# A fused cross-attention and token-mixing kernel rewritten: casting loads, state read in head groups under a mask, keys made per token, three batches in one loop

## The chip, the cores and the metric

The kernel runs on one core of a Trainium2 chip. The metric is the device time of one execution in microseconds, as the median of several runs. A profile is one more execution, with the hardware's own record of every instruction; its span goes from the first to the last instruction on the core.

## What is computed

Inputs are x (8 batches, 8 heads, 512 tokens, 64 wide), state (8, 8, 32, 64) and three weight matrices. First comes attention both ways between x and state, for each batch and head; then the two results are put together into 544 tokens of 512 features, and these are mixed across tokens.

```python
scores = scale * x @ state.T                      # 512 x 32 for each head
a = softmax(scores, over the 32 state rows)
xread = a @ state                                 # 512 x 64
a2 = softmax(scale * state @ x.T, over the 512 tokens)
sread = a2 @ x                                    # 32 x 64
y = concat([xread, sread]) as 544 x 512           # heads side by side
wq, wk = y @ w_q, y @ w_k                         # 544 x 64
mixed = (scale * wq @ wk.T) @ y                   # 544 x 512
out = relu(mixed) @ w_out                         # 544 x 512
```

## The kernel before, in words

No softmax subtracts its maximum. One exponent E serves both directions: summed over state rows and divided it gives A, the weights of xread; multiplied with x and a column of ones it gives sread and its sums. xread itself is never formed. Since it is A times state, the kernel multiplies state with w_q and w_k once (SW) and A^T with that. In the mixing, wk^T y (64 x 512, "V") is made first, through G, the product of A and the keys, and a block-diagonal state "stbd"; then mixed = wq V.

Setup, before the batches: w_out, w_q and w_k come in by SP's queue as f32 (L66 to L76), and GpSimd casts them to bf16 (L67, L80, L81). For each batch state comes as 32 partitions (L85), ScalarE casts it (L87), VectorE writes its eight blocks into stbd one by one (L94, 64 copies in all), and TensorE transposes it and multiplies it with the weights (L102 to L134).

Then a loop over eight batches, each written as one straight line. x comes in as f32 (L141, 1 MB a batch, tokens on partitions). VectorE casts it twice: x_sd with a column of ones for sread (L143, L147) and x_sd2 with pairs of heads side by side (L152). TensorE transposes that 16 times (L157), ScalarE copies the result (L163, L164), 16 matmuls make the scores pt_ps (L169). ScalarE takes the exponent E_sn (L177), VectorE sums and inverts (L179, L181), GpSimd multiplies to A_sn (L183). Eight transposes make A^T (L193, copied at L199); 32 matmuls of 65 columns make sread head by head (L206), which VectorE normalises (L217, L218) and TensorE transposes (L227, L233). Then wqk (L237, L245: queries and keys at once, feature layout, copied at L253), the keys turned back by five transposes (L258, L263, copied at L269, L270), g (L275, L283), v (L286, L290, V at L298), four mixS and four narrow mixT32 matmuls (L303, L310) with relu to rmix (L317, L324), sixteen fin matmuls of 512 columns (L336, copied at L343) and one output of 1 MB (L344). After every fourth batch the 32 state tokens of four batches go through w_out together (L352 to L361).

Tiles double up (pool pb has two buffers of each), and the tile framework sets all waits and the order on each engine: it takes instructions in the order written, and lets a ready one of the next batch ahead where an engine and a buffer are free. `nc.any` copies go to ScalarE or VectorE at its choice. The instruction order below is what it made.

Of the kernel before, what the change touches and what calls it, by code (L numbers as in the profile page):

```python
# [8 lines left out]
FP = mybir.dt.float32  # L10
BF = mybir.dt.bfloat16
AF = mybir.ActivationFunctionType
ALU = mybir.AluOpType
# [4 lines left out]
def kernel(  # L18
# [14 lines left out]
    SP = S + NS  # L33
    DH = moe_w_q.shape[1]
    NG = 4
    SG = S // NG
    KC = DM // 128
    HG = H // 4
    NP = H // 2
    scale = 1.0 / float(D) ** 0.5  # L40
# [3 lines left out]
    persist = ctx.enter_context(tc.tile_pool(name="persist", bufs=1))  # L44
    pb = ctx.enter_context(tc.tile_pool(name="pb", bufs=2))
    rmixp = ctx.enter_context(tc.tile_pool(name="rmixp", bufs=1))
    outstg = ctx.enter_context(tc.tile_pool(name="outstg", bufs=3))
    psA = ctx.enter_context(tc.tile_pool(name="psA", bufs=2, space=bass.MemoryType.PSUM))
    psB = ctx.enter_context(tc.tile_pool(name="psB", bufs=1, space=bass.MemoryType.PSUM))
    psC = ctx.enter_context(tc.tile_pool(name="psC", bufs=3, space=bass.MemoryType.PSUM))  # L50

    ident = const.tile([128, 128], BF, name="ident")
    make_identity(nc, ident)
    ident64hi = const.tile([128, 64], BF, name="ident64hi")
    nc.gpsimd.memset(ident64hi, 0.0)
    make_identity(nc, ident64hi[64:128, :], nomemset=True)

    state_sb = []
    stbd_sb = []
    stT2_sb = []  # L60
    SW_sb = []

    with tc.tile_pool(name="wstage", bufs=1) as wstage:
        w_out_sb = persist.tile([128, KC, DM], BF, name="w_out_sb")
        wo_stage = wstage.tile([128, KC, DM], FP, name="wo_stage")
        nc.sync.dma_start(out=wo_stage, in_=moe_w_out.rearrange("(k p) e -> p k e", p=128))  # L66
        nc.gpsimd.tensor_copy(out=w_out_sb, in_=wo_stage)  # L67

        w_qk_sb = persist.tile([128, NP, 2 * DH], BF, name="w_qk_sb")
        wq_stage = wstage.tile([128, NP, DH], FP, name="wq_stage")  # L70
        wk_stage = wstage.tile([128, NP, DH], FP, name="wk_stage")
        nc.sync.dma_start(
            out=wq_stage,
            in_=moe_w_q.rearrange("(q2 hp d) j -> hp d q2 j", q2=NP, hp=2),
        )
        nc.sync.dma_start(  # L76
            out=wk_stage,
            in_=moe_w_k.rearrange("(q2 hp d) j -> hp d q2 j", q2=NP, hp=2),
        )
        nc.gpsimd.tensor_copy(out=w_qk_sb[:, :, 0:DH], in_=wq_stage)  # L80
        nc.gpsimd.tensor_copy(out=w_qk_sb[:, :, DH : 2 * DH], in_=wk_stage)  # L81

        for b in range(B):
            stf = wstage.tile([NS, H, D], FP, name="stf", tag="stf", bufs=2)
            nc.sync.dma_start(out=stf, in_=state[b].rearrange("h n d -> n h d"))  # L85
            st_sb = persist.tile([NS, H, D], BF, name=f"state_sb{b}")
            nc.scalar.copy(out=st_sb, in_=stf)  # L87
            state_sb.append(st_sb)

            stbd = persist.tile([128, HG, 4 * D], BF, name=f"stbd{b}")  # L90
            nc.gpsimd.memset(stbd, 0.0)
            for h in range(H):
                g, k = h // 4, h % 4
                nc.vector.tensor_copy(  # L94
                    out=stbd[32 * k : 32 * k + 32, g, D * k : D * k + D],
                    in_=st_sb[:, h, :],
                )
            stbd_sb.append(stbd)

            stT2_ps = psC.tile([128, NP, NS], BF, name="stT2_ps", tag="psC")  # L100
            for q in range(NP):
                nc.tensor.transpose(  # L102
                    out=stT2_ps[:, q, :],
                    in_=st_sb[:, 2 * q : 2 * q + 2, :],
                    identity=ident[0:NS, 0:NS],
                )
            stT2 = persist.tile([128, NP, 2 * NS], BF, name=f"stT2_sb{b}")
            nc.gpsimd.memset(stT2, 0.0)
            nc.any.tensor_copy(out=stT2[0:64, :, 0:NS], in_=stT2_ps[0:64, :, :])
            nc.any.tensor_copy(  # L110
                out=stT2[64:128, :, NS : 2 * NS], in_=stT2_ps[64:128, :, :]
            )
            stT2_sb.append(stT2)

            swt_ps = psC.tile([128, NP, 2 * NS], FP, name="swt_ps", tag="psC")
            for q in range(NP):
                nc.tensor.matmul(  # L117
                    out=swt_ps[:, q, :],
                    lhsT=w_qk_sb[:, q, :],
                    rhs=stT2[:, q, :],  # L120
                    start=(q == 0),
                    stop=(q == NP - 1),
                )
            swt = wstage.tile([128, NP, 2 * NS], BF, name="swt", tag="swt", bufs=2)
            nc.any.tensor_copy(out=swt, in_=swt_ps)
            sw_ps = psC.tile([128, HG, 2 * DH], BF, name="sw_ps", tag="psC")
            for g in range(HG):
                nc.tensor.transpose(
                    out=sw_ps[:, g, :],
                    in_=swt[:, 2 * g : 2 * g + 2, :],  # L130
                    identity=ident,
                )
            sw = persist.tile([128, HG, 2 * DH], BF, name=f"SW_sb{b}")
            nc.any.tensor_copy(out=sw, in_=sw_ps)  # L134
            SW_sb.append(sw)

    rmix = rmixp.tile([128, KC, B * SP], BF, name="rmix")

    for b in range(B):
# [3 lines left out]
        nc.vector.tensor_copy(  # L143
            out=x_sd[:, :, :, 0:D],
            in_=xf32.rearrange("p h (c d) -> p h c d", c=NG),
        )
        nc.gpsimd.memset(x_sd[:, :, :, D : D + 1], 1.0)  # L147
        x_sd2 = pb.tile([128, NG, 2 * D * NP], BF, name="x_sd2")
        x_sd2_v = x_sd2.rearrange("p c (q hp d) -> p c q hp d", q=NP, hp=2)
        xf32_v = xf32.rearrange("p (q hp) (c d) -> p c q hp d", q=NP, hp=2, c=NG)  # L150
        for hp in range(2):
            nc.vector.tensor_copy(out=x_sd2_v[:, :, :, hp, :], in_=xf32_v[:, :, :, hp, :])  # L152

        xT_ps = psA.tile([128, NP, NG, SG], BF, name="xT_ps", tag="psA")
        for q in range(NP):
            for c in range(NG):
                nc.tensor.transpose(  # L157
                    out=xT_ps[:, q, c, :],
                    in_=x_sd2[:, c, 128 * q : 128 * q + 128],
                    identity=ident,  # L160
                )
# [230 lines left out]
```

## Time and profile before

| | us |
|---|---|
| runs | 183.29 median (182.05 to 183.35, 3 runs) |
| profiled execution, span | 179.0 |
| TensorE busy | 126.7 (71%) |
| ScalarE busy | 90.2 (50%) |
| VectorE busy | 69.5 (39%) |
| GpSimd busy | 31.2 (17%) |
| mean granted TensorE clock | 0.82 |

Busy time of TensorE includes the time that a pipelined matmul is under way, so it is not work at full rate. "PEclk" is the clock granted to TensorE, in tenths of full speed or as a share. In groups, "idle before" is the time that the engine stood free just before these instructions, and what ended it.

### The profile page before, as it was taken

To read this page: it belongs to the slowest core of one execution; us is meant where nothing else is said; L and a number is where in the kernel's file an instruction comes from. 1 tells how busy PE (TensorE), PEld (TensorE's weight loads), DVE (VectorE), ACT (ScalarE), POOL (GpSimd) and SP (SyncE) were. 2 spreads that over 40 slices of the span, in tenths; PEclk is the share of its full clock that TensorE was granted. 3 is DMA by queue.
4 is the path that set the end of the run, shared out by engine and by line. 5 is a ranking of instruction groups with operands and counts; after the bars stand their busy time and mean duration, and the time that the engine had idled before them with its cause. 6 is when DMAs were issued, how large, how long until landed. Compare 5 with 4: busy or idle time off the path is not lost.

```text
span 179.0 us, 2649 instructions
## 1 busy us (share of the span) xinstructions
PE 126.7 (71%) x1064; PEld 68.4 (38%) x1064; DVE 69.5 (39%) x172; ACT 90.2 (50%) x159; POOL 31.2 (17%) x43
## 2 busy tenths in 40 slices
PE   0020656689995897699679967996899789848800
PEld 0010535464254434443453345445535533522300
DVE  0099979985616403440434043404140350203000
ACT  2130574477465744663477446744666673543600
POOL 3592003100411040004302130033021004000000
PEclk9999999999999759756995795579558975975985
DMA  5992071076019303900580061005000500320061
GB/s 148 302 275 94 15 247 25 12 234 224 17 59 302 111 0 156 296 17 4 205 264 0 4 240 53 0 4 234 0 0 4 234 0 2 150 88 0 29 222 42
DMA packets 13507, 19.29 MB, mean 108 GB/s; under 512 B 3512, under 2 KB 11704, under 8 KB 12472
## 3 DMA queue, kind: packets, MB, share of 16 engines
q1 hardware_dynamic: 13496, 19.14, 31.8%
q8 instruction: 8, 0.13, 0.3%
q14 instruction: 3, 0.02, 0.0%
HBM read 10.22 MB, written 8.91 MB: 107 GB/s over the span
## 4 chain that ended last, share of the span: by engine, by line
PE 56%; DVE 18%; ACT 13%; DMA 3%; issue 3%; POOL 1%; SPq 1%; ACTq 0%; DVEq 0%; POOLq 0%
PE fin_ps L336 23%; DVE stbd L94 8%; PE mixS_ps L303 7%; PE srd_ps L206 6%; DMA stf<-in_state_dram 3%; DVE x_sd L143 3%; DVE sread_sb L218 3%; PE pt_ps L169 3%; ACT E_sn L177 3%; PE xT_ps L157 3%; PE at_ps L193 2%; PE v_ps L286 2%; ACT xT_sb L163 2%; PE v_ps L290 2%; ACT wqkT_sb L253 2%
## 5 line engine op out<-in xcount | busy, mean ns | idle before, releaser
L336 PE MATMUL fin_ps<-w_out_sb,rmix 128*128 128x512 bf16 x128 | 42.2, 501 | 0.0
L343 ACT COPY ostage<-fin_ps 128x512 f32<-128x512 f32 x32 | 18.8, 586 | 23.3 <-PE fin_ps L336 23.0
L183 POOL TENSOR_TENSOR A_sn<-E_sn,rinv 128x1024 bf16<-128x1024 bf16 x8 | 15.5, 1941 | 76.0 <-DVE rinv L181 75.0
L336 PEld LDWEIGHTS <-rmix 128*128 128x128 bf16 x128 | 15.0, 124 | 26.7 <-issue 20.7
L94 DVE COPY stbd<-state_sb 32x64 bf16<-32x64 bf16 x64 | 17.5, 274 | 10.5 <-POOL w_qk_sb L81 9.1
L217 DVE RECIPROCAL rinv<-srd_ps 32x4 f32<-32x4 f32 x16 | 2.6, 161 | 46.5 <-PE srd_ps L206 46.5
L303 PE MATMUL mixS_ps<-wqkT_sb,V_sb 64*128 64x512 bf16 x32 | 17.4, 587 | 1.3 <-ACT V_sb L298 1.2
L317 ACT ACTIVATE rmix<-mixS_ps 128x512 bf16<-128x512 f32 x23 | 13.6, 597 | 5.0 <-PE mixS_ps L303 4.3
L206 PE MATMUL srd_ps<-x_sd,E_sn 128*32 128x65 bf16 x256 | 14.0, 210 | 1.7 <-ACT E_sn L177 1.4
L317 DVE TENSOR_SCALAR rmix<-mixS_ps 128x512 bf16<-128x512 f32 x9 | 6.2, 692 | 21.1 <-PE mixS_ps L303 21.1
L206 PEld LDWEIGHTS <-E_sn 128*32 128x32 bf16 x256 | 10.7, 105 | 7.0 <-issue 3.5
L152 DVE CAST x_sd<-xf 128x1024 bf16<-128x1024 f32 x16 | 10.8, 680 | 6.3 <-PE xT_ps L157 6.3
L147 POOL MEMSET x_sd<- 128x32 bf16 x8 | 6.4, 821 | 37.7 <-PE srd_ps L206 37.7
L157 PE MATMUL xT_ps<-ident,x_sd 128*128 128x128 bf16 x128 | 12.3, 254 | 0.0
L169 PE MATMUL pt_ps<-stT_sb,xT_sb 128*128 128x64 bf16 x128 | 8.9, 224 | 3.0 <-ACT xT_sb L163 2.9
L179 DVE TENSOR_REDUCE rsum<-E_sn 128x32 f32<-128x1024 bf16 x8 | 9.7, 1211 | 1.2 <-ACT E_sn L177 1.2
L143 DVE CAST x_sd<-xf 128x2048 bf16<-128x2048 f32 x8 | 9.6, 1204 | 0.0
L233 ACT COPY srT_sb<-srT_ps 128x128 bf16<-128x128 bf16 x8 | 2.1, 266 | 14.5 <-PE srT_ps L227 14.5
L157 PEld LDWEIGHTS <-x_sd 128*128 128x128 bf16 x128 | 9.2, 114 | 0.3
L102 PE MATMUL stT_ps<-ident,state_sb 32*128 32x32 bf16 x32 | 2.3, 188 | 10.0 <-POOL w_qk_sb L81 9.0
L163 ACT COPY xT_sb<-xT_ps 128x1024 bf16<-128x1024 bf16 x8 | 8.1, 1012 | 1.8 <-PE xT_ps L157 1.8
L117 PE MATMUL swt_ps<-stT_sb,w_qk_sb 128*128 128x64 bf16 x32 | 3.1, 239 | 8.1 <-ACT stT_sb L110 8.1
(67 smaller groups left out, 158.1 us busy)
## 6 DMA issues: line engine op xcount, KB each, us to landing
xf<-in_x_dram SPq DMA_DIRECT2D x8, 1024.0 KB, 5.7
out_dram<-ostage SPq DMA_DIRECT2D x8, 1024.0 KB, 3.9
wo_stage<-in_moe_w_out_dram SPq DMA_DIRECT2D x1, 1024.0 KB, 5.5
stf<-in_state_dram SPq DMA_DIRECT2D x8, 64.0 KB, 2.1
out_dram<-ostage SPq DMA_DIRECT2D x2, 256.0 KB
wq_stage<-in_moe_w_q_dram SPq DMA_DIRECT2D x1, 128.0 KB, 5.6
wk_stage<-in_moe_w_k_dram SPq DMA_DIRECT2D x1, 128.0 KB, 5.7
```

The costliest lines, as they stand in the source:

```text
L94: nc.vector.tensor_copy(out=stbd[32 * k : 32 * k + 32, g, D * k : D * k + D], in_=st_sb[:, h, :],)
L143: nc.vector.tensor_copy(out=x_sd[:, :, :, 0:D], in_=xf32.rearrange("p h (c d) -> p h c d", c=NG),)
L152: nc.vector.tensor_copy(out=x_sd2_v[:, :, :, hp, :], in_=xf32_v[:, :, :, hp, :])
L157: nc.tensor.transpose(out=xT_ps[:, q, c, :], in_=x_sd2[:, c, 128 * q : 128 * q + 128], identity=ident,)
L163: nc.any.tensor_copy(out=xT_sb[:, 0:2], in_=xT_ps[:, 0:2])
L169: nc.tensor.matmul(out=pt_ps[:, c, 2 * q : 2 * q + 2, :], lhsT=xT_sb[:, q, c, :], rhs=stT2_sb[b][:, q, :], start=(q == 0 and c % 2 == 0), ...
L183: nc.gpsimd.tensor_tensor(out=A_sn, in0=E_sn, in1=rinv[:, :, :, None].to_broadcast((128, NG, H, NS)), op=ALU.mult,)
L206: nc.tensor.matmul(out=srd_ps[:, g, 65 * hh : 65 * hh + 65], lhsT=E_sn[:, c, h, :], rhs=x_sd[:, h, c, :], start=(hh == 0 and c == 0), stop ...
L303: nc.tensor.matmul(out=mixS_ps, lhsT=V_sb[:, 128 * k : 128 * k + 128], rhs=wqT_sb[:, 0:S], start=True, stop=True,)
L317: nc.any.tensor_scalar(out=rmix[:, k, S * b : S * b + S], in0=mixS_ps, scalar1=0.0, scalar2=None, op0=ALU.max,)
L336: nc.tensor.matmul(out=fin_ps, lhsT=rmix[:, k, S * b + SG * c : S * b + SG * c + SG], rhs=w_out_sb[:, k, :], start=(k == 0), stop=(k == KC ...
L343: nc.any.tensor_copy(out=ostage[:, c, :], in_=fin_ps)
```

## The change

The kernel is written anew, with the same arithmetic. On the inputs:

- x (two loads a batch, four heads each), w_q, w_k and w_out are loaded by GpSimd's queue, and the transfer casts them from f32 to bf16. All of x has its own place in SBUF (x_bf0 to x_bf7), and all 19 loads are issued at the start. State comes in one load of 128 partitions. All casts of x on VectorE and of weights on GpSimd are gone.
- state's copies, transposes and stbd are made for all batches at once, with head h = 4r + q at partition group q of half r: four stbd copies, sixteen transposes, four weight products of 512 columns.

In a batch:

- s_xT transposes x_bf with two tokens of a group of four side by side, so no copy in another layout is needed; s_pt multiplies with state in two interleaved copies. VectorE, not ScalarE, copies xT and A^T.
- s_srd multiplies the E of four heads with x of four heads and a block of ones: eight matmuls of 128 x 320 in place of 32 of 32 x 65. Only the blocks on the diagonal are wanted: VectorE multiplies by the inverse sum and a mask in one scalar_tensor_tensor. s_srT sums over partition groups by a stacked identity, as it transposes.
- s_wqk makes queries in feature layout as before, and keys directly per token, by twelve matmuls of 64 columns; the five transposes back are gone.
- s_mix takes queries of real and state tokens together, 2 x 272 columns, so the narrow matmuls and their relu are gone. fin's results leave in pairs of token groups: copies of 1024 columns, all on ScalarE, and outputs of 512 KB.

The loop runs over ten iterations. Iteration i works on batch X = i (xT, pt, srd), Y = i - 1 (at, srT, wqk, g, v) and Z = i - 2 (mix, fin), and the stages of the three are written between one another. PSUM is two pools, psA with three tiles of two banks and psB with two of one.

GpSimd's queue, from the start of the program to the second A ("[waits ...]" names the semaphores; DMASW0 to DMASW7 count the landings of loads, taken in turn). Before:

```order
L67 CAST w_out_sb<-wo_stage 128x2048
L80 CAST w_qk_sb<-wq_stage 128x4x64
L81 CAST w_qk_sb<-wk_stage 128x4x64
...
L147 MEMSET x_sd 128x32 x3
L183 TENSOR_TENSOR A_sn<-E_sn,rinv 128x1024 x2
```

Now:

```order
L66 DMA x_bf_73<-in_x_dram 128x4x256 x2
L75 DMA w_qk<-in_moe_w_q_dram 128x4x64
L78 DMA w_qk<-in_moe_w_k_dram 128x4x64
...
L83 DMA w_o<-in_moe_w_out_dram 128x4x512
L66 DMA x_bf_75<-in_x_dram 128x4x256
L66 DMA x_bf_75<-in_x_dram 128x4x256 [waits DMASW0_49]
L66 DMA x_bf_76<-in_x_dram 128x4x256 [waits DMASW1_49]
...
L66 DMA x_bf_80<-in_x_dram 128x4x256 [waits DMASW2_49]
L194 TENSOR_TENSOR A<-E,rinv 128x1024 [waits DVE_49,Activation_49] x2
```

The loads moved from SP's queue to GpSimd's, ahead of every A; from the ninth load on each one waits for the landing of the load eight before it.

ScalarE's queue over one batch of the steady part. Before:

```order
L199 COPY AT_sb<-at_ps 128x1024
L233 COPY srT_sb<-srT_ps 128x128
L253 CAST wqkT_sb<-wqk_ps 128x544
L163 COPY xT_sb<-xT_ps 128x1024
L270 COPY wkt_sb<-wkt_ps 32x64
L164 COPY xT_sb<-xT_ps 128x1024
L298 ACTIVATE V_sb<-v_ps 64x512
L177 ACTIVATE E_sn<-pt_ps 128x1024
L317 ACTIVATE rmix<-mixS_ps 128x512
L324 ACTIVATE rmix<-mixT_ps 128x4x32
L317 ACTIVATE rmix<-mixS_ps 128x512 x2
L343 COPY ostage<-fin_ps 128x512 x4
```

Now:

```order
L344 ACTIVATE rmix<-mix_ps 128x544 x3
L185 ACTIVATE E<-pt_ps 128x1024
L274 CAST wq<-wq_ps 64x544
L367 COPY ost<-fin_ps 128x1024
L328 ACTIVATE V<-v_ps 64x512
L367 COPY ost<-fin_ps 128x1024
```

The copies of A^T, xT, srT and keys left ScalarE for VectorE; the exponent of batch X now stands between the relu and the outputs of batch Z, and V of batch Y between the two outputs.

TensorE in one steady iteration now stands so (counts of matmuls in a row): 8 xT, 2 mix, 6 at, 2 mix, 8 xT, 2 at, 4 mix, 4 srT, 16 pt, 4 fin, 6 wq, 12 wk, 4 fin, 8 srd, 2 fin, 8 g, 2 fin, 3 v, 4 fin.

The core of the diff:

```diff
-        xf32 = pb.tile([128, H, NG * D], FP, name="xf32")
-        nc.sync.dma_start(out=xf32, in_=x[b].rearrange("h (p c) d -> p h c d", c=NG))
-        x_sd = pb.tile([128, H, NG, D + 1], BF, name="x_sd")
...
+    psA = ctx.enter_context(tc.tile_pool(name="psA", bufs=3, space=bass.MemoryType.PSUM))
+    psB = ctx.enter_context(tc.tile_pool(name="psB", bufs=2, space=bass.MemoryType.PSUM))
+    x_bf = [xin.tile([128, 2, NP + 1, NC * D], BF, name=f"x_bf{b}") for b in range(B)]
...
+    def load_x(b):
+        for r in range(2):
+            nc.gpsimd.dma_start(
+                out=x_bf[b][:, r, 0:NP, :],
+                in_=x[b, NP * r : NP * r + NP].rearrange("h (p c) d -> p h (c d)", c=NC),
+            )
+
+    nc.sync.dma_start(
+        out=st_f, in_=state.rearrange("b (r q) n d -> (q n) (b r) d", r=2)
+    )
+    load_x(0)
...
+    load_x(1)
+    nc.gpsimd.dma_start(out=w_o, in_=moe_w_out.rearrange("(k p) e -> p k e", p=128))
+    for b in range(2, B):
+        load_x(b)
...
+    nc.vector.tensor_copy(
+        out=st_bf, in_=st_f[:, :, :, None, :].to_broadcast((128, B, 2, 2, D))
+    )
...
+    def s_xT(b):
...
+                nc.tensor.transpose(
+                    out=ps[:, u, h, :],
+                    in_=x_bf[b][:, h // NP, h % NP, 128 * u : 128 * u + 128],
+                    identity=ident,
+                )
+            nc.vector.tensor_copy(out=xT[:, u], in_=ps[:, u])
...
+    def s_srd(b):
...
+            for c in range(NC):
+                nc.tensor.matmul(
+                    out=ps,
+                    lhsT=L["E"][:, c, r, :, :],
+                    rhs=x_bf[b][:, r, :, D * c : D * c + D],
+                    start=(c == 0),
+                    stop=(c == NC - 1),
+                )
+            nc.vector.reciprocal(out=rinv2[:, r : r + 1], in_=ps[:, NP, 0:1])
+            nc.vector.scalar_tensor_tensor(
+                out=sbd[:, r, :, :],
+                in0=ps[:, 0:NP, :],
+                scalar=rinv2[:, r : r + 1],
+                in1=mask[:, :, None].to_broadcast((128, NP, D)),
+                op0=ALU.mult,
+                op1=ALU.mult,
+            )
...
+    def s_wqk(b):
...
+        for c in range(NC):
+            for r in range(2):
+                nc.tensor.matmul(
+                    out=psk[:, c, :],
+                    lhsT=L["AT"][:, r, c, :],
+                    rhs=sw[:, b, r, DH : 2 * DH],
+                    start=(r == 0),
+                    stop=(r == 1),
+                )
...
+    def s_mix(b, k, eng):
+        L = live[b]
+        ps = psA.tile([128, 2, 512], FP, name="mix_ps", tag="psA")
+        for h in range(2):
+            nc.tensor.matmul(
+                out=ps[:, h, 0:HALF],
+                lhsT=L["V"][:, 128 * k : 128 * k + 128],
+                rhs=L["wq"][:, HALF * h : HALF * h + HALF],
+                start=True,
+                stop=True,
+            )
...
+    for i in range(B + 2):
+        X, Y, Z = i, i - 1, i - 2
+        hx, hy, hz = X < B, 0 <= Y < B, 0 <= Z
+        if hx:
+            s_xT(X)
+        if i == 0:
+            setup_sw()
+        if hz:
+            s_mix(Z, 0, "act")
+            s_mix(Z, 1, "dve")
+        if hy:
+            s_at(Y)
+        if hz:
+            s_mix(Z, 2, "act")
+            s_mix(Z, 3, "act")
+            nc.gpsimd.tensor_copy(out=rmix_s[:, Z // 4, :, Z % 4, :], in_=rmix[:, Z, :, S:SP])
+        if hx:
+            s_pt(X)
+        if hz:
+            s_fin_mm(Z, 0)
+        if hy:
+            s_srT(Y)
+            s_wqk(Y)
+        if hz:
+            s_fin_mm(Z, 1)
+            s_fin_out(Z, 1, "act")
+        if hx:
+            s_srd(X)
+        if hy:
+            s_g(Y)
+        if hz:
+            s_fin_mm(Z, 2)
+        if hy:
+            s_v(Y)
+        if hz:
+            s_fin_mm(Z, 3)
+            s_fin_out(Z, 3, "act")
+            if Z % 4 == 3:
+                s_fin_s(Z // 4)
```

More of the change, by code (lines that the diff above doesn't have):

```diff
@@ L131 @@
                     identity=ident,
                 )
[L133 to L139, printed above, removed]
[L140 to L156 removed]
+        stT_v = stT_ps.rearrange("p b r (q n) -> p b (r q) n", q=NP)
@@ new lines, in s_v @@
+    def s_v(b):
+        L = live[b]
+        ps = psB.tile([DH, 2, NP, D], FP, name="v_ps", tag="psB")
+        nc.tensor.matmul(
+            out=ps, lhsT=L["wk"][:, NC, :], rhs=L["sbd"], start=True, stop=False
+        )
+        for r in range(2):
+            nc.tensor.matmul(
+                out=ps[:, r, :, :],
+                lhsT=L["G"][:, r, :],
+                rhs=stbd[:, b, r, :, :],
+                start=False,
+                stop=(r == 1),
+            )
+        V = work.tile([DH, DM], BF, name="V")
+        nc.scalar.mul(out=V, in_=ps.rearrange("p r q d -> p (r q d)"), mul=float(scale2))
+        L["V"] = V
```

460 lines of the change are left out of this document (212 added, 248 removed).

## The prediction

> **What bounds the kernel now.** I read the page first: engines, slices, chain.
>
> ```profile
> span 179.0 us, 2649 instructions
> ...
> PE 126.7 (71%) x1064; PEld 68.4 (38%) x1064; DVE 69.5 (39%) x172; ACT 90.2 (50%) x159; POOL 31.2 (17%) x43
> ...
> PEclk9999999999999759756995795579558975975985
> ...
> GB/s 148 302 275 94 15 247 25 12 234 224 17 59 302 111 0 156 296 17 4 205 264 0 4 240 53 0 4 234 0 0 4 234 0 2 150 88 0 29 222 42
> ...
> HBM read 10.22 MB, written 8.91 MB: 107 GB/s over the span
> ...
> PE 56%; DVE 18%; ACT 13%; DMA 3%; issue 3%; POOL 1%; SPq 1%; ACTq 0%; DVEq 0%; POOLq 0%
> ```
>
> No engine is full. TensorE is busiest, at 71%, and holds 56% of the chain; VectorE and ScalarE hold 31% more, though they are busy only 39% and 50%. So it is not one engine's work that ends last but a chain that passes from engine to engine. The GB/s row falls near zero between bursts, so DMA bounds nothing. The clock row dips again and again from the fourteenth slice on.
>
> Next the chain in order of time, for one batch:
>
> ```profile
> 120.67 0.45 PE at_ps L193 x8
> 121.12 0.92 PE srd_ps L206 x25
> ...
> 128.76 0.56 PE v_ps L290 x2
> 129.33 0.87 PE pt_ps L169 x14
> ...
> 133.11 4.63 PE fin_ps L336 x16
> 137.74 0.45 PE at_ps L193 x8
> ```
>
> Five more rows of the chain, for the steps on the start, the clock and the end below:
>
> ```profile
> 0.73 0.45 SPq L66
> ...
> 2.32 5.99 DMA stf<-in_state_dram
> ...
> 29.97 1.92 POOL A_sn L183
> ...
> 47.22 4.48 PE fin_ps L336 x14
> ...
> 168.41 0.88 PE fin_ps L352 x4
> ```
>
> From at_ps to the next at_ps is 17.07 us: the period of one batch. From at_ps to the end of v_ps (129.3) the chain hops through attention copies, key transposes, g and v in 8.7 us. Only one batch's fin_ps, 4.63 us, is dense work. Eight such periods are three quarters of the span. Last I read the period in stretches of 3.4 us (columns: stretch, length, then busy time and count for PE, PEld, DVE, ACT, POOL, granted clock, DMA share, GB/s):
>
> ```profile
> 118.20:121.60 3.40, 3.40 (x37) 1.99 (x36) 0.00 (x0) 2.65 (x5) 0.00 (x0) 1.00 0.00 0
> 121.60:125.00 3.40, 1.96 (x32) 1.27 (x29) 2.11 (x5) 0.88 (x2) 1.38 (x1) 1.00 0.74 308
> 125.00:128.40 3.40, 2.53 (x30) 1.85 (x26) 0.76 (x3) 2.64 (x3) 0.00 (x0) 0.50 0.00 0
> 128.40:131.80 3.40, 3.30 (x27) 1.71 (x26) 1.04 (x2) 2.10 (x4) 0.00 (x0) 0.50 0.00 0
> 131.80:135.20 3.40, 3.40 (x12) 1.12 (x12) 1.13 (x2) 1.38 (x4) 1.91 (x1) 0.50 0.00 0
> 135.20:138.60 3.40, 3.40 (x35) 2.00 (x34) 0.00 (x0) 2.58 (x5) 0.00 (x0) 0.99 0.02 5
> ```
>
> A stretch with PE busy 1.96 of 3.40 us (58%) is followed by three at clock 0.50; after two nearly full ones (3.30 and 3.40) it is 1.00 again. The hand-overs cost twice: as idle time, and as half speed afterwards, when the next dense work comes.
>
> **The change part by part.** *Steady state.* In each iteration three batches stand between one another on TensorE, so one batch's hand-over is filled by another's matmuls. What is left is TensorE's own time. Paces at full clock:
>
> ```profile
> 166.00:169.30 3.30, 2.40 (x11) 0.88 (x9) 1.00 0.00 0
> ```
>
> This row is fin_ps (L336) alone, busy time and count of PE and PEld, then clock: 11 matmuls of 512 columns in 2.40 us, 0.218 each, so 0.43 ns a column. A 128-column transpose is at_ps's 0.45 / 8 = 0.056, and a small one srd_ps's 0.92 / 25 = 0.037 (both rows above). An iteration after has: 16 xT, 8 at and 4 srT of 128 columns, 28 x 0.056 = 1.57; 16 pt, 12 wk, 8 g and 4 narrow wq, 40 x 0.037 = 1.48; 2 wq, 0.44; v, 0.44; 8 srd of 320 columns (they replace 32 of 65), 8 x 0.136 = 1.09; 8 mix of 272, 8 x 0.116 = 0.93; 16 fin, 3.49. Sum 9.44 us.
>
> The other engines, by the groups of instructions on ScalarE, on VectorE and on GpSimd (the last two numbers ahead of the idle time are busy us and mean ns):
>
> ```profile
> L177 ACT ACTIVATE E_sn<-pt_ps 128x1024 bf16<-128x1024 f32 x8 | 8.2, 1024 | 1.0 <-PE pt_ps L169 1.0
> L163 ACT COPY xT_sb<-xT_ps 128x1024 bf16<-128x1024 bf16 x8 | 8.1, 1012 | 1.8 <-PE xT_ps L157 1.8
> ...
> L253 ACT CAST wqkT_sb<-wqk_ps 128x544 bf16<-128x544 f32 x8 | 4.9, 612 | 2.7 <-PE wqk_ps L245 2.7
> ...
> L298 ACT ACTIVATE V_sb<-v_ps 64x512 bf16<-64x512 f32 x8 | 4.7, 591 | 7.6 <-PE v_ps L290 7.6
> ```
>
> ```profile
> L179 DVE TENSOR_REDUCE rsum<-E_sn 128x32 f32<-128x1024 bf16 x8 | 9.7, 1211 | 1.2 <-ACT E_sn L177 1.2
> L143 DVE CAST x_sd<-xf 128x2048 bf16<-128x2048 f32 x8 | 9.6, 1204 | 0.0
> L218 DVE TENSOR_TENSOR sread_sb<-srd_ps,rinv 32x256 bf16<-32x256 f32 x16 | 6.5, 407 | 0.3
> L317 DVE TENSOR_SCALAR rmix<-mixS_ps 128x512 bf16<-128x512 f32 x9 | 6.2, 692 | 21.1 <-PE mixS_ps L303 21.1
> L181 DVE RECIPROCAL rinv<-rsum 128x32 f32<-128x32 f32 x8 | 2.8, 352 | 0.7
> ...
> L164 DVE COPY xT_sb<-xT_ps 128x1024 bf16<-128x1024 bf16 x1 | 0.7, 680 | 0.0
> ```
>
> ```profile
> L183 POOL TENSOR_TENSOR A_sn<-E_sn,rinv 128x1024 bf16<-128x1024 bf16 x8 | 15.5, 1941 | 76.0 <-DVE rinv L181 75.0
> ```
>
> ScalarE per iteration: exponent 1.02, wq 0.61, V 0.59, three rmix of 544 at 0.61, two output copies of 1024 at 1.01: 6.1 us. VectorE: three bf16 copies at 0.68, sum 1.21, reciprocal 0.35, two head-group reads at 0.41 (scalar_tensor_tensor is new; the nearest row is L218) with two small reciprocals, at most 0.35 together, srT and rmix at about 0.69, and wk and G of 320 and 128 columns, by the share of columns 0.43 and 0.17: 6.4 to 6.9 us. The three casts of x (1.20 and two half-size ones) are gone; they lay on the chain as "x_sd". GpSimd: 1.94 and a small copy. All three stay under 9.4, so TensorE bounds, and those removals are worth nothing beyond that.
>
> TensorE still waits where three two-bank tiles go round through xT, mix, pt and fin: the mix tiles wait for relu. Below: about 0.3 an iteration, one wait. Above: 2.4 us, the difference of 17.07 and the most that the engine stood free in a period (1.44 + 0.87 + 0.10 us in the six stretches). I take 1.0, since three mix hand-overs remain and the rest has other matmuls between. Iteration: 10.4 us. What hides the hand-overs of wk, g and v are fin's four groups, which stand between them; without that cover each costs what it does now, 8.7 us in all, and V, for which all mix waits, would be late next.
>
> *Clock.* 9.44 of 10.4 us is 91% busy, far from the 58% that was followed by half clock. But the program starts at half speed: the fourteen fin_ps at 47.2 us took 0.32 each, against 0.22 at clock 1.00, though the page's clock row shows 9 there. The first dense work in the new order meets it too: two stretches at half speed, about 7 us, lose 3.5. [...] The rows above show two busy ones at 0.50 before 1.00, so 3.5 stands.
>
> *Start.* State comes in one load, and x and the weights come cast, in 19 loads that GpSimd issues. Its first A stands behind all 19; and loads 9 to 19 each wait until the load eight before has landed. So A(0) waits for load 11: x of four batches 4.19 MB, the weights 1.31, and state's 0.52 beside them on another queue, 6.0 MB. How fast casting loads run, no row shows. The nearest are the first ten us (columns as above) and the loads' time from issue to landing:
>
> ```profile
> 0.00:10.00 10.00, 0.28 (x4) 0.18 (x4) 0.94 (x1) 2.86 (x5) 5.09 (x16) 1.00 0.86 242
> ```
>
> ```profile
> xf<-in_x_dram SPq DMA_DIRECT2D x8, 1024.0 KB, 5.7
> ...
> stf<-in_state_dram SPq DMA_DIRECT2D x8, 64.0 KB, 2.1
> ```
>
> The first ten us moved 242 GB/s; one x load alone, 1.05 MB in 5.7 us, 184. I take the middle, 213: 28.2 us. With 1 us to the first issue, 2.1 for a small landing, 0.5 for the last issue and 1.94 for A, A(0) stands at 34 us. Bounds: 308 GB/s (a stretch above) gives 25; 150, should the cast cost a quarter or GpSimd's issue take longer than SP's 0.45, gives 46 to 48. The data chain itself is done sooner: state landed at 8.3 us before (the row at 2.32); its cast 1.2, sixteen transposes at half speed 1.8, copies out of PSUM near 2.2, two of xT 1.4, pt 0.9, exponent 1.0, sum 1.2, reciprocal 0.35 and some 2 us of hand-overs end near 20. So the queue sets the start. Casting on arrival saves nothing here: before, A(0) was ready at 31.9 (the row at 29.97). Later x is no limit: 10.22 MB at 213 is in at 51 us, and x(7) is wanted near 98.
>
> [...]
>
> *Iteration 1* is A(0) to V(0), the 8.7 us chain, at half clock without its x_sd: 9. *Iteration 8* lacks xT, pt and srd (0.90 + 0.59 + 1.09): 7.8. *Iteration 9* has mix, three relus in line on ScalarE (0.3 + 1.83 + 0.2), fin 3.49 and the last group 0.87: 7. *Tail*: before, PE ends at 169.3 and the span at 179.0, 9.7 us; the last transfer is now half as large, 0.5 MB at 222 GB/s less, so 8 with what hangs on it.
>
> Sum: 34 + 9 + 6 x 10.4 + 3.5 + 7.8 + 7 + 8 = 131.8 us of span. The median of the runs, 183.29, is 4.3 over the profiled span. 131.8 + 4.3 = **136 us**.
>
> **The rivals.** *Slow casting loads.* If a casting packet takes twice as long (106 GB/s), A(0) stands at 62 and the time is 136 + 28 = 164. For it: 16-bit targets make packets of 512 B, and no row has a cast. Against: the read, 1 KB, is what it was.
>
> *The clock keeps falling.* mix, xT and at carry short matmuls and relu waits together. If one window each iteration falls under the mark, two at half speed follow: 3.4 us lost, 6 x 3.4 = 20, time 156. For it: 58% is close to what that section may reach with waits of 2 us. Against: one such wait is 0.3.
>
> *Loads bound everything, slower than before.* Casting element by element: x(7) must be in by 183.3 - 4.3 - (10.4 + 7.8 + 7 + 8) = 146 us, so the mechanism decides from 10.2 MB / 146 = 70 GB/s down. At 60 it is 170 + 33 + 4 = 207 us. Against: it takes a fourfold loss.
>
> *The three batches do not overlap*, the order holding one stage for the next as now: 34 + 9 + 6 x 17.1 + 14.5 (17.1 less 2.6) + 9.5 (fin partly at half speed) + 8 + 4.3 = 182 us. Against: no stage's input is made less than two groups of matmuls ahead.
>
> **How the numbers follow.** Forecast 0.65, slow loads 0.12, falling clock 0.13, loads bound 0.05, no overlap 0.05. Forecast's own range: start -9 / +14, waits 7 x (-0.7 / +1.4), not both at their ends, 124 to 154. To hold 8 in 10 it runs from 122 to 162, into the falling clock and slow loads. Faster by over 1% (what a measurement of this kernel can just tell from nothing): the first three, 0.90. Within 1%: no overlap, 0.05. Slower: 0.05.
>
> **What would show it.** The first A on GpSimd near 32, behind 19 loads; TensorE's period near 10.4 with clock 1.00 from about 50 us; fin_ps near 0.22 each; ScalarE and VectorE near 6 to 7 us a period; about 8 us after the last matmul. Wrong would be: GpSimd free well before the sum is ready, a clock row with 5s past the middle, or a gap before xT for want of x.

## The result, and the profile after

Measured beside each other, the changed kernel took 119.35 us (118.86 to 119.63, 4 runs) and the kernel before 183.12 us (182.05 to 183.35, 4 runs): ratio 0.654, 95% interval 0.649 to 0.658. The forecast was 136.0, with 122 to 162 as range. The direction was right; the time lies below the range.

The page of the changed kernel, the same rows as before:

```profile
span 117.8 us, 2155 instructions
...
PE 91.4 (78%) x884; PEld 54.4 (46%) x884; DVE 67.3 (57%) x138; ACT 57.4 (49%) x80; POOL 33.1 (28%) x41
...
PEclk9999999999999999999999999999999999999955
...
GB/s 73 199 155 188 202 196 196 196 196 195 37 0 6 17 161 178 6 178 132 46 58 125 178 0 181 171 58 43 178 178 6 178 81 97 149 213 32 333 53 27
...
q0 software_dynamic: 10032, 4.85, 31.3%
...
PE 70%; DVE 17%; ACT 2%; issue 2%; POOL 2%; ACTq 0%; DVEq 0%; POOLq 0%
```

TensorE alone now holds 70% of the chain (56% before), and ScalarE, which held 13%, holds 2%. The clock row has no dip until the work is done; that the start ran at half speed (0.47 us for a matmul of 512 columns at 17.55) it does not show (see the cold clock below). One period of the steady state (columns as in the prediction):

```profile
53.07:63.22 10.15, 10.15 (x109) 5.95 (x106) 6.52 (x13) 5.87 (x8) 2.20 (x2) 1.00 0.26 105
```

TensorE is busy in all of a period of 10.15 us, at clock 1.00; VectorE 6.5, ScalarE 5.9, GpSimd 2.2. That is the forecast's picture (10.4; 6.4 to 6.9; 6.1; about 2.2). Where it went otherwise most is the start. The chain in order of time up to the first A:

```profile
3.89 1.78 DVE stbd L93
...
9.50 0.48 DVE x_bf L95
...
9.98 1.43 DVE st_bf L102
...
11.46 1.05 PE stT_ps L110 x8
12.53 0.29 DVE stT L117
...
17.55 1.86 PE swT_ps L132 x4
19.41 0.33 PE sw_ps L146 x2
19.74 0.80 PE pt_ps L177 x15
20.54 1.49 PE sw_ps L146 x14
...
24.99 0.33 DVE rinv L192
...
25.46 1.92 POOL A L194
```

and GpSimd's own queue, its last load and that A (in brackets its idle time and what ended it):

```profile
20.39 0.74 POOL L66 DMA_DIRECT2D x_bf<-in_x_dram  x1 [0.66 <-DMA x_bf<-in_x_dram]
25.46 1.91 POOL L194 TENSOR_TENSOR A<-E,rinv 128x1024 bf16<-128x1024 bf16 x1 [4.33 <-DVE rinv L192]
```

GpSimd was through with its 19 loads at 21.1 us and then stood idle 4.33 us for the sum, one of the signs of being wrong that the prediction had named. So the data chain set the start, not the queue. On that chain VectorE filled stbd and then the eight columns of ones (4.3 us for the eight, the last at 9.50) before it cast the state at 9.98. The stT copies, which alternate between VectorE and ScalarE, ran from 12.5 to 17.5 us with the two copies of xT(0) between them. Then the set-up's own matmuls (swT, and sixteen transposes to sw) stood ahead of the last of the sixteen pt matmuls until 22.0.

The forecast's terms against the profile (A(0) ready; A(0) to the first mix; six periods with the clock's loss; iterations 8 and 9; the tail after TensorE's last matmul):

| term | forecast | measured | difference |
|---|---|---|---|
| start, A(0) ready | 34 | 27.4 | -6.6 |
| iteration 1, to 34.3 | 9 | 6.9 | -2.1 |
| six iterations, to 94.7 | 62.4 + 3.5 | 60.4 | -5.5 |
| iteration 8, to 102.7 | 7.8 | 8.0 | +0.2 |
| iteration 9, to 109.0 | 7 | 6.3 | -0.7 |
| tail, to 117.8 | 8 | 8.8 | +0.8 |
| median over profiled span | 4.3 | 1.6 | -2.7 |

### The profile page after: what moved, and what is told of

It is laid out like the page before. It is cut to its first block, busy times and chain, and to the rows that moved or that the text cites. A ratio compares the mean times of both kernels' runs of the same rounds, so it can differ in the third digit from the quotient of the medians.

```text
span 117.8 us, 2155 instructions
## 1 busy us (share of the span) xinstructions
PE 91.4 (78%) x884; PEld 54.4 (46%) x884; DVE 67.3 (57%) x138; ACT 57.4 (49%) x80; POOL 33.1 (28%) x41
## 3 DMA queue, kind: packets, MB, share of 16 engines
q1 hardware_dynamic: 4632, 9.44, 21.3%
## 4 chain that ended last, share of the span: by engine, by line
PE 70%; DVE 17%; ACT 2%; issue 2%; POOL 2%; ACTq 0%; DVEq 0%; POOLq 0%
PE fin_ps L356 25%; PE mix_ps L335 8%; PE xT_ps L163 6%; PE srd_ps L221 6%; PE wq_ps L258 3%; PE at_ps L207 3%; DVE x_bf L95 3%; PE pt_ps L177 3%; PE v_ps L316 2%; DVE xT L168 2%; PE wk_ps L278 2%; DVE rsum L190 2%; PE srT_ps L243 2%; POOL A L194 2%; PE swT_ps L132 2%
## 5 line engine op out<-in xcount | busy, mean ns | idle before, releaser
L356 PE MATMUL fin_ps<-w_o,rmix 128*128 128x512 bf16 x128 | 34.0, 381 | 0.0
L194 POOL TENSOR_TENSOR A<-E,rinv 128x1024 bf16<-128x1024 bf16 x8 | 15.3, 1910 | 25.4 <-DVE rinv L192 17.9
L367 ACT COPY ost<-fin_ps 128x1024 f32<-128x1024 f32 x16 | 16.2, 1012 | 9.3 <-PE fin_ps L356 7.8
L163 PE MATMUL xT_ps<-ident,x_bf 128*128 128x128 bf16 x128 | 11.6, 237 | 9.4 <-DMA x_bf<-in_x_dram 7.3
L344 ACT ACTIVATE rmix<-mix_ps 128x544 bf16<-128x544 f32 x24 | 14.1, 623 | 6.0 <-PE mix_ps L335 6.0
L168 DVE COPY xT<-xT_ps 128x1024 bf16<-128x1024 bf16 x16 | 10.9, 684 | 9.4 <-PE xT_ps L163 9.4
L66 POOL DMA_DIRECT2D x_bf<-in_x_dram x16 | 12.8, 806 | 5.3 <-DMA x_bf<-in_x_dram 2.7
L190 DVE TENSOR_REDUCE rsum<-E 128x32 f32<-128x1024 bf16 x8 | 9.8, 1220 | 5.5 <-ACT E L185 5.5
L335 PE MATMUL mix_ps<-wq,V 64*128 64x272 bf16 x64 | 10.8, 279 | 0.7 <-ACT ost L367 0.6
L185 ACT ACTIVATE E<-pt_ps 128x1024 bf16<-128x1024 f32 x8 | 8.2, 1024 | 5.9 <-PE pt_ps L177 5.8
L221 PE MATMUL srd_ps<-x_bf,E 128*128 128x320 bf16 x64 | 10.2, 299 | 0.0
## 6 DMA issues: line engine op xcount, KB each, us to landing
x_bf<-in_x_dram POOLq DMA_DIRECT2D x16, 256.0 KB, 10.4
```

The source lines that it names most:

```text
L66: nc.gpsimd.dma_start(out=x_bf[b][:, r, 0:NP, :], in_=x[b, NP * r : NP * r + NP].rearrange("h (p c) d -> p h (c d)", c=NC),)
L163: nc.tensor.transpose(out=ps[:, u, h, :], in_=x_bf[b][:, h // NP, h % NP, 128 * u : 128 * u + 128], identity=ident,)
L168: nc.vector.tensor_copy(out=xT[:, u], in_=ps[:, u])
L185: nc.scalar.activation(out=E, in_=ps.rearrange("p c r (q n) -> p c r q n", q=NP), func=AF.Exp, scale=float(scale))
L190: nc.vector.reduce_sum(out=rsum, in_=Ev, axis=AX.X)
L194: nc.gpsimd.tensor_tensor(out=A.rearrange("p c r q n -> p (c r q) n"), in0=Ev, in1=rinv[:, :, None].to_broadcast((128, NC * 2 * NP, NS)), ...
```

## The experiments

The theory going in: the interleaving of three batches is the gain; it fills the hand-overs and keeps the clock. The rival: the new instructions (casting loads, wider and fewer matmuls) are the gain. Beside it stood the misses: what sets the start, and what the cold clock costs.

### Less interleaving

The first run keeps every stage and writes them batch after batch:

```
-    for i in range(B + 2):
-        X, Y, Z = i, i - 1, i - 2
+    for b in range(B):
+        s_xT(b); s_pt(b); s_at(b); s_srd(b); s_srT(b); s_wqk(b)
+        s_g(b); s_v(b); s_mix(b, 0, "act"); ...; s_fin_mm(b, c)
```

> The changed kernel's stages unchanged (casting loads, masked read, token-layout keys, same instructions), but written batch after batch, so that TensorE does no work of another batch while a batch's chain of copies runs. Theory (the interleaving of three batches is most of the gain): TensorE waits some 7 to 8 us in each batch for E, A, AT, wk, G, V and rmix; the period goes from 10.15 to 17 to 19 us and the clock leaves 1.00 again: 165 to 190 us. Rival (the shorter and fewer instructions are the gain, the order is worth little): period 11 to 12 us, 125 to 135 us.

The second has two batches in the loop: all attention of batch i, with mix and fin of batch i - 1 between.

```
-        X, Y, Z = i, i - 1, i - 2
+        X, Z = i, i - 1
```

> The changed kernel with a loop over two batches in place of three: the attention of a batch, from xT to V, in one iteration, and only mixing and output of the batch before as filling work. Theory (overlap sets the period): the chain of one batch, about 5.5 us of TensorE and some 7 us of copies between, no longer fits into 10.15 us, of which the other batch fills about half of the gaps: period 11.5 to 13 us, one iteration less: 125 to 138 us. Rival (TensorE alone sets the period, any second batch fills the gaps): period 10.2 and one iteration less at the end: 112 to 118 us.

Measured: batch after batch 217.3 us (ratio to before 1.192, interval 1.184 to 1.200), two batches 145.8 us (0.802, 0.796 to 0.808). The first went past the theory's own range, the second is above it by 8 us; both are far from the rival. The page of the first:

```profile
span 215.6 us, 2144 instructions
...
PE 127.5 (59%) x876; PEld 70.1 (33%) x884; DVE 72.4 (34%) x138; ACT 58.1 (27%) x80; POOL 33.1 (15%) x41
...
PEclk9999999957887576958597666958596767858595
```

Against the changed kernel, TensorE is busy 36.1 us longer with the same matmuls (127.5 less 91.4) and idle 61.7 us longer (88.1 less 26.4). Together that is the whole difference of the spans, 97.8: by estimate from these two numbers a bit over a third is half clock, the rest idle hand-overs. (The mean granted clock is 0.776 against 0.974, and the same matmuls are busy longer: fin 41.2 us against 34.0, srd 18.7 against 10.2, mix 14.5 against 10.8.) How the one makes the other, in stretches of 3.4 us (laid so that the changes of the clock in the trace fall on their bounds):

```profile
112.20:115.70 3.50, 1.25 (x24) 1.00 (x23) 1.19 (x3) 1.02 (x1) 0.00 (x0) 0.99 0.55 174
115.70:119.10 3.40, 0.00 (x0) 0.00 (x0) 1.36 (x2) 0.00 (x0) 1.79 (x1) 0.50 0.15 59
119.10:122.50 3.40, 3.22 (x18) 2.13 (x18) 1.36 (x4) 0.00 (x0) 0.12 (x1) 0.50 0.00 0
```

After a stretch with TensorE busy 1.25 us the clock is 0.50; while E, its sum and A are made TensorE does nothing; the dense stretch after it (3.22 us) still runs at 0.50. And by groups, the same 128 matmuls of fin:

```profile
L356 PE MATMUL fin_ps<-w_o,rmix 128*128 128x512 bf16 x120 | 41.2, 501 | 1.4 <-ACT rmix L344 1.3
```

501 ns each, as in the kernel before, against 381 in the changed one (below). The two-batch loop, one of its periods:

```profile
45.73:59.32 13.59, 10.87 (x106) 6.18 (x105) 6.59 (x13) 5.80 (x9) 2.20 (x2) 1.00 0.19 77
```

In this period the clock stays at 1.00, and 2.7 us of 13.6 are idle. V(0) starts at the same time as in the changed kernel (33.4 and 33.6 us), V(7) 27.8 us later (129.5 and 101.8): the whole difference. So the gain needs the interleaving: without it the new instructions are slower than the kernel before. The other half of the comparison, the old instructions in the interleaved order, was not run. As TensorE's own work fills the period now, its shorter matmuls may have a share in the gain that is not shown.

### The start

Two set-up moves. First the ones columns leave the set-up:

```
-    for b in range(B):
-        nc.vector.memset(x_bf[b][:, :, NP, :], 1.0)
...
+        nc.vector.tensor_scalar(out=x_bf[b][:, :, NP, :], in0=xT[:, 1, 0:4, :]...,
+            scalar1=0.0, scalar2=1.0, op0=ALU.mult, op1=ALU.add)
```

> The eight memsets of the ones columns (4.3 us on VectorE ahead of the state's cast) are taken out of the set-up; each batch's ones are made from its xT copy instead, as x times 0 plus 1, in its own iteration. Theory (VectorE's set-up chain, state cast to stT to swT to pt(0) to A(0), sets the start, not GpSimd's load issues): the state's cast starts at about 5.7 instead of 9.9 us, the stT copies then wait for ScalarE's stbd casts, which end at 10.5, instead of 12.85: A(0) starts 2 to 4.3 us earlier, end 115 to 117.5 us. Rival (the sixteen loads on GpSimd's queue, free at 21.1 us, or their arrival set the start): less than 1 us, 118.5 to 119.5.

Then, on top of it, ScalarE's stbd casts go behind pt(0):

```
-        nc.scalar.copy(out=stbd[blk, :, :, q, :], in_=st_f[blk])
...
+        nc.scalar.activation(out=stbd[blk, :, :, q, :], in_=st_f[blk], func=AF.Copy, scale=one[blk])
```

> As the run before, and ScalarE's four stbd casts (4.2 us and ahead of its stT copies) wait for a scalar made from sw, so that they follow pt(0)'s exponential. Theory (the data chain): stT, swT and pt(0) come 4 to 6 us earlier than in the changed kernel, until GpSimd's queue of loads, free at 21.1 us, takes over as the bound: A(0) starts at 21.1 instead of 25.5 us, end about 114 to 116 us. Rival (the loads' arrival or the clock, opened later by the set-up's thinner window, gives it back): 117 to 119.5 us.

Measured: 117.6 us each (ratios 0.644, 0.638 to 0.651; and 0.646, 0.640 to 0.652). The first is the theory's direction, just past its range: A(0) began at 22.83 in place of 25.46. The second gained nothing more, as its rival said. Its chain in order of time shows why:

```profile
10.51 10.47 DMA x_bf<-in_x_dram
...
21.27 0.17 POOL x_bf L66
...
22.02 1.93 POOL A L205
24.00 0.64 PE at_ps L218 x8
```

and the stretches behind it:

```profile
22.20:25.60 3.40, 1.27 (x21) 1.12 (x22) 2.85 (x5) 3.01 (x4) 1.74 (x1) 1.00 1.47 201
25.60:29.10 3.50, 3.50 (x27) 2.14 (x26) 2.00 (x4) 0.92 (x2) 0.00 (x0) 0.51 1.44 193
```

The data were ready at 21.4, and now GpSimd's loads end last: the predicted mechanism, at 22.0 us and not at 32. And the earlier start left a hole in TensorE's work (1.27 us of 3.40) which closed the clock for one stretch: from the start of at(0) to V(0) it took 8.0 us, where it took 6.2 in the changed kernel.

Each of the two was then taken away. A(0) alone made by VectorE, past GpSimd's queue:

```
-        nc.gpsimd.tensor_tensor(
+        (nc.vector if b == 0 else nc.gpsimd).tensor_tensor(
```

> The run with both set-up moves (ones columns and stbd casts), and the first batch's A made by VectorE instead of GpSimd, whose queue of loads ended only at 22.0 us there. Theory (in that run two things gave the earlier start back: A(0) waited for GpSimd's loads, and the hole in TensorE's work at 22.2 to 25.6 us closed the clock for one window): A(0) is ready near 22.7 instead of 23.9, the hole is shorter; with the clock kept 113.5 to 115.5 us. Rival (the clock closes all the same, or the later casts on VectorE give the 1.2 us back): 116 to 117.6 us.

and twenty more transposes in the hole:

```
+        if b == 0:
+            for w in range(20):
+                nc.tensor.transpose(out=ps[:, w % 2, w // 2 % NC, :], in_=L["xT"][:, 1, w % H, :], identity=ident)
```

> The run with A(0) on VectorE, and twenty transposes more on TensorE, of data it has, into the at tile ahead of the real ones, in the hole where it waits for A(0) (21.5 to 22.7 us); their results are overwritten. Nothing else is changed: work is added. Theory (the hole closed the clock for one window there, 24.4 to 27.8 us, and this costs up to 1.7 us): the windows list 1.00 from some 17.6 us to the end, and the end comes 1 to 2 us earlier, 113.8 to 115 us against 115.9. Rival (the copies and not TensorE's clock set iteration 1, or the added transposes delay at(0)): 115.7 to 117.5 us.

The first: 115.9 us (115.1 to 116.8; ratio 0.637, 0.629 to 0.644), between the two expectations. V(0) comes 1.3 us sooner than in the run before it and the end 1.6; the clock still closed. The second, in its profile, held the clock. The same place in both:

```profile
21.00:24.40 3.40, 1.89 (x33) 1.43 (x31) 3.40 (x9) 3.35 (x4) 0.76 (x2) 1.00 1.45 198
24.40:27.80 3.40, 3.28 (x24) 1.88 (x24) 2.64 (x5) 1.44 (x2) 0.13 (x1) 0.50 1.46 195
```

```profile
19.80:23.20 3.40, 3.30 (x58) 2.81 (x56) 3.40 (x10) 3.36 (x4) 1.16 (x2) 1.00 1.46 199
23.20:26.60 3.40, 2.96 (x37) 2.04 (x35) 3.20 (x7) 1.91 (x3) 0.01 (x1) 1.00 1.44 193
```

From the start of at(0) to V(0) it took 6.8 us (21.96 to 28.74) where the run before took 8.1 (22.67 to 30.74): 1.3 us for one cold stretch. But the median of its six runs, 115.8 us (ratio 0.634, 0.630 to 0.639), is that of the run without the transposes: the rival's number. Its runs lie at 114.9 (two, one of them profiled) and 115.5 to 116.0 (four), and the clock changes at other times from profile to profile (at 25.6 and 29.1 us in the run with both set-up moves, at 24.4 and 27.8 with A(0) on VectorE); whether the slower four missed the clock is not shown (their mean granted clock, 0.971 to 0.984, is not below the 0.965 of the fastest two). Either version beats the changed kernel by some 3%.

### The cold clock

The changed kernel's set-up without the sixteen sw transposes that fill one stretch (sw is a plain copy):

```
-                    nc.tensor.transpose(out=ps[:, bb, r, :], in_=swT[...], identity=ident)
-                nc.scalar.copy(out=sw[:, bs], in_=ps)
+                nc.scalar.copy(out=sw[:, bs], in_=swT[:, bs]...)
```

> The changed kernel without the sixteen sw transposes of the set-up (sw is a plain copy of swT, so its values are not the reference's); all else is the same. They are the work that fills the window 19.5 to 22.9 us, after which the clock opens. Theory (one full window of some 3.4 us opens the clock, and where it is not full the start runs at half speed): the work itself saves 1.5 us, but the clock opens one or two windows later, which costs 1.7 to 3.4 us in iteration 1: 119 to 121.5 us, and the windows list 0.50 up to some 30 us. Rival (half speed in the start costs nothing, since the copies and not TensorE set iteration 1): 116.5 to 118.3 us.

Measured 120.6 us (120.1 to 122.1; ratio 0.663, 0.655 to 0.671): less work, and some 1.3 us longer, the theory's number. The intervals of the two ratios just overlap (0.649 to 0.658 for the changed kernel), the single runs do not (at most 119.63 there). Its stretches, and those of the changed kernel at the same place:

```profile
22.10:25.50 3.40, 3.40 (x30) 2.44 (x28) 2.34 (x6) 0.00 (x0) 0.00 (x0) 1.00 1.45 196
25.50:28.90 3.40, 1.00 (x16) 0.81 (x14) 2.53 (x5) 1.02 (x1) 1.91 (x1) 1.00 1.45 196
28.90:32.30 3.40, 3.31 (x25) 1.88 (x25) 1.33 (x4) 0.61 (x1) 1.91 (x1) 0.50 0.40 56
```

```profile
19.50:22.90 3.40, 3.40 (x40) 3.27 (x39) 1.33 (x2) 1.69 (x3) 0.98 (x2) 1.00 1.45 196
22.90:26.30 3.40, 1.96 (x25) 1.50 (x23) 3.29 (x8) 0.36 (x1) 0.84 (x1) 1.00 1.45 196
26.30:29.70 3.40, 1.95 (x30) 1.42 (x31) 1.97 (x4) 1.02 (x1) 1.07 (x1) 1.00 1.44 197
```

The clock column lists 1.00 from 16.10 to 19.50 us already, though in the changed kernel four swT matmuls of 512 columns took 1.86 us at 17.55 (0.47 each, quoted above; 0.218 each at clock 1.00 in the prediction). So the start's half speed is read from durations: eight transposes of x took 1.01 us at 15.17, 1.04 at 21.89 and 0.61 at 30.59, and the eight at_ps transposes 0.62 at 27.43. The stretch from 16.10 to 19.50 had TensorE busy 2.03 of 3.40 us, the one from 19.50 to 22.90 all of 3.40. One full stretch opened the clock here, and the two busy ones at 0.50 that the prediction took from its rows did not carry over. Without the transposes the full stretch came 2.6 us later, and a hole (1.00 of 3.40) closed the clock once more, to 0.50 in the next stretch. So a cold stretch does cost 1.3 to 1.8 us (the two comparisons above), but the changed kernel's set-up pays it, before the iterations begin.

How full a stretch must be is not shown. In the kernel before, one with TensorE busy 3.30 of 3.40 us did not open the clock (the prediction's row at 128.40). Nor does the busy share tell when it closes: after 1.96 of 3.40 it closed in the kernel before, after 1.89 in the run with A(0) on VectorE, and after 1.96 and 1.95 it stayed open in the changed kernel (rows above). So the prediction's 58% was no mark that carries from one kernel to the next.

### Casting on arrival

x loaded as f32 by SP, cast by VectorE:

```
-            nc.gpsimd.dma_start(out=x_bf[b][:, r, 0:NP, :], in_=...)
+        nc.sync.dma_start(out=t, in_=x[b]...)
...
+        nc.vector.tensor_copy(out=x_bf[b][:, :, 0:NP, :], in_=x_f[b]...)
```

> The changed kernel with x loaded as float32 by SP (1 MB a load, four staging buffers) and cast by VectorE, one cast of 2048 columns a batch ahead of xT; the weights still come cast by GpSimd. Theory (casting on arrival saves VectorE work that is not on the path, since TensorE sets the period): VectorE goes from some 6.9 to 8.1 us of a 10.15-us period, which stays, and the start changes by less than 3 us: 116 to 123 us. Rival (the cast on VectorE stands ahead of xT and its 1.2 us show in each of eight batches): 128 to 130 us.

Measured 128.8 us (127.0 to 130.5; ratio 0.700, 0.689 to 0.710): near the rival's number, but not by its mechanism. From V(0) on, the starts of V lie apart exactly as in the changed kernel; V(0) itself is late, at 41.3 instead of 33.6 us. VectorE's queue in the set-up:

```profile
16.08 1.23 DVE L160 CAST x_bf<-x_f 128x2048 bf16<-128x2048 f32 x1 [2.64 <-DMA x_f<-in_x_dram]
17.23 0.47 DVE L118 COPY stT<-stT_ps 64x256 bf16<-64x256 bf16 x2
...
19.09 1.23 DVE L160 CAST x_bf<-x_f 128x2048 bf16<-128x2048 f32 x1 [0.40 <-DMA x_f<-in_x_dram]
```

The scheduler put casts of later batches ahead of the stT copies, and VectorE waited there for loads that nothing needed yet. So a second version tied each cast to its own iteration, and the loads of batches 4 to 7 as well:

```
+            nc.vector.tensor_scalar(out=one, in0=live[b - 1]["xT"][:, 1, 0, 0:1], scalar1=0.0, scalar2=1.0, ...)
+            nc.vector.tensor_scalar(out=x_bf[b][:, :, 0:NP, :], in0=x_v, scalar1=one, ..., op0=ALU.mult)
```

> As the run with x loaded uncast by SP and cast by VectorE, but each cast of batches 1 to 7 multiplies by a one made from the batch before's xT, so that it stands in its own iteration and not in the set-up. Theory (in that run the casts cost 7.6 us because they stood in VectorE's queue ahead of the set-up's copies and waited for their loads; inside an iteration VectorE has room for 1.2 us more): the starts of V lie 10.1 to 10.4 us apart as in the changed kernel, V(0) comes by 36 us, 118.5 to 122 us. Rival (a cast ahead of xT shows in each iteration): the period grows by 0.7 to 1.2 us and the time is 126 to 130 us.

Measured 119.8 us (118.7 to 120.2; ratio 0.657, 0.647 to 0.667), the changed kernel's time. One period:

```profile
52.15:62.30 10.15, 10.05 (x106) 6.04 (x105) 7.69 (x15) 5.87 (x8) 2.21 (x3) 1.00 0.25 103
```

VectorE has 1.2 us more, 7.69, and the period is 10.15 as before. So loading x cast is worth nothing here that these runs can tell from noise; the weights still came cast.

### The pace of loads

Four batches of x, 1.05 MB each, loaded cast by GpSimd, then uncast by GpSimd, then by SP. All else is left out; what is loaded is written out.

> Loads alone, all other work left out: four batches of x (4.19 MB as float32) loaded three times, one after the other: cast to bfloat16 by GpSimd's queue, uncast by GpSimd's queue, uncast by SP's queue; then the output is written from what was loaded. Theory (a casting load moves its halved destination bytes at the usual rate, so that counting its source bytes at 213 GB/s made the start too late): the cast phase takes 10 to 13 us (330 to 420 GB/s of source), the two uncast ones 17 to 22 us each (190 to 240 GB/s). Rival (the 213 GB/s was only too low for any queue full of loads, and casting has no part in it): all three phases take 11 to 14 us.

A small VectorE copy marks each batch's landing, first the cast ones (from xa), then the uncast (from xb):

```profile
11.34 0.17 DVE L46 CAST gate<-xa 128x2 f32<-128x2 bf16 x1 [2.01 <-DMA xa<-in_x_dram]
...
16.69 0.17 DVE L46 CAST gate<-xa 128x2 f32<-128x2 bf16 x1 [2.29 <-DMA xa<-in_x_dram]
...
26.47 0.17 DVE L46 COPY gate<-xb 128x2 f32<-128x2 f32 x1 [2.55 <-DMA xb<-in_x_dram]
...
32.37 0.17 DVE L46 COPY gate<-xb 128x2 f32<-128x2 f32 x1 [2.52 <-DMA xb<-in_x_dram]
```

Two cast batches in 5.35 us are 392 GB/s of source bytes (196 of destination, the number that stands in the changed kernel's GB/s row); two uncast ones in 5.90 us are 355. The rival was right that casting has no part in it: kept full, GpSimd's queue moved 392 GB/s of source in this run with the cast and 355 without. Counted from the first issue the two phases took 15.5 and 15.0 us, a little over its 11 to 14: the first batch took 7.4 and 5.9 to land. Of SP's loads this run shows 273 to 365 GB/s in the three full slices ahead of the writes.

## Why the prediction was right, and where it failed

**Right.** What bounds the kernel, the hand-overs and the clock that follows them: taking the interleaving away from the new instructions brought both back (61.7 us more of idle time, a mean granted clock of 0.776); for the kernel before it is read from its trace. The iteration, forecast at 10.4 us, took 10.15. Its two parts stand less firmly: the trace has TensorE busy in all of the 10.15, so the 1.0 of waits does not show as idle time, and where the 0.7 us above the sum of 9.44 lie is not shown. The clock at 1.00, the other engines under the period, the removed casts worth nothing, iteration 8, iteration 9 and the tail within 0.8 us: as forecast. None of the rivals came. (The terms of the forecast's sum add up to 131.7, not 131.8.)

**The start: the failed step.** "I take the middle, 213: 28.2 us" and "so the queue sets the start" were both wrong. 213 was the mean of a single load's time to landing and of ten us that include the first issue; the loads alone ran at 355 and 392. At 21.1 us the queue was done. The data chain, put near 20, took until 25.3. Three things made it longer. VectorE's list holds stT2, stbd and eight ones columns ahead of the state's cast, which began at 9.98, though the state was there at 5.0 (forecast: 8.3). The set-up's own matmuls on the chain, swT and sw, 3.7 us at half speed, were in no term; the run without sw's transposes shows that taking them out alone does not bring A(0) sooner (25.62), since on VectorE copies of the next batch then stand ahead of the sum. And the copies of stT and xT(0), costed at 2.2 and 1.4, took 5.0 together, handed between two engines. The other terms came out 1.8 shorter. So the queue was forecast 11 us too late and the chain 5 too early, and A(0) was hung on the wrong one; that the term missed by 6.6 and not by more is luck.

**The cold clock.** "Two stretches at half speed, about 7 us, lose 3.5" fell: after the start, the clock cost the changed kernel nothing, because the set-up's own matmuls open it at 22.9 us, and because one full stretch was enough there. The 9 us of iteration 1 held half clock once more ("at half clock"): 6.9 measured, at full clock. So half clock stood in two terms that came out 5.6 us too long, and had no lower bound in the range. How much of iteration 1's 2.1 is the clock alone is not shown; a cold stretch there cost 1.3 to 1.8 in the runs above. The rest of the six iterations' difference, 2.0 us: the first took 8.7 us, since the start had done part of its work; the others took 10.15 in place of 10.4; against that stands 0.9 for the first state rows' output, which the sum had left out.

**The median's offset.** "The median of the runs, 183.29, is 4.3 over the profiled span" took a chance for a constant. In the runs here, the time of the profiled execution is 1.8 us over its span in each of three kernels (119.63 and 117.8; 217.37 and 215.6; 147.06 and 145.3). So before's profiled execution took about 180.8, 2.5 us under its median.

**GpSimd beside VectorE.** The traces show instructions of GpSimd and VectorE that took longer where the two worked beside each other, and the forecast's sum had no term for it. In the changed kernel the load that GpSimd issued at 10.33, beside VectorE's cast of the state, took 1.38 us where its neighbours took 0.74; that cost nothing, as the queue did not set the start. Where the ones columns were moved, the same cast came at 5.57 and met GpSimd's making of the identity matrix. That instruction in the changed kernel, and in the run with both set-up moves:

```profile
5.34 0.34 POOL masks.py:199 TENSOR_SCALAR_AFFINE_SELECT ident<-ident 128x128 bf16<-128x128 bf16 x1
...
5.34 1.54 POOL masks.py:199 TENSOR_SCALAR_AFFINE_SELECT ident<-ident 128x128 bf16<-128x128 bf16 x1
```

It took 1.2 us more, in a run where that queue did set the start, and the queue was through at 22.0, not at 21.1. And in that run VectorE's small copy of ones took 0.32 us while GpSimd only issued loads, and 1.45 us beside A:

```profile
12.59 0.32 DVE L175 TENSOR_SCALAR x_bf<-xT 128x512 bf16<-128x512 bf16 x1
22.66 1.45 DVE L175 TENSOR_SCALAR x_bf<-xT 128x512 bf16<-128x512 bf16 x1
```

It ended at 24.1, A at 23.9. What made these instructions longer is not shown.

## What to carry to other kernels

Interleaving batches paid twice here: about a third of what its removal cost (36.1 of 97.8 us, the estimate above) was half clock, not idle time, and the new instructions without it were slower than the old kernel. Before a load queue is named as the bound of a start, its pace is to be taken from a stretch in which it is full, and everything that stands in an engine's list ahead of the first needed operation (memsets, the set-up's matmuls, casts for later batches) counts with it. A correction that has only one profiled execution behind it, such as the offset to the median or a cold clock, needs its own bound down to zero in the range.

## What was not expected of the hardware

- The same 128 matmuls of 512 columns took 501 ns each with the clock coming and going, and here, in the changed kernel, 381:

```profile
L356 PE MATMUL fin_ps<-w_o,rmix 128*128 128x512 bf16 x128 | 34.0, 381 | 0.0
```

- Adding work can cost nothing and taking work away can cost time: twenty transposes more in the start left the median where it was (115.8 and 115.9 us), and sixteen less in the set-up made the kernel some 1.3 us slower.
- In the run of loads alone the casting loads were a little faster by their source bytes than the uncast ones (392 and 355 GB/s), and the GB/s row counts their destination bytes: 192 to 197 in its full slices.
- GpSimd was busy 0.81 us with each of its sixteen x loads, 12.8 in all, where SP issued a load in 0.45 in the kernel before (the prediction's row at 0.73).
